# Reordering a block-sorted attention and token-mixing MLP kernel: attention of two batches one unit sooner, token units two later, an affine in single steps

## The chip, the cores and the metric

The kernel runs on one core of a Trainium2 chip. The metric is the device time of one execution in microseconds (us). A change of the order of instructions only is made; the arithmetic and the number of bytes moved are the same before and after.

## The reference

Two parts run one after the other, for 4 batches (S = 768 rows, 8 heads of 64, model width 512, hidden width 2048):

```
P = sinkhorn(sort_net, 5 rounds)                  # 8 x 8 per batch and head
k_sorted = P applied to the 8 blocks of k;  v_sorted = the same of v   # blocks of 96 rows
scores = q_b @ k_sorted_b^T / 8                   # within a block: 96 x 96
x = softmax(scores) @ v_sorted_b                  # heads side by side: 768 x 512
a1 = alpha1 * x + beta1
u  = x + lam * (w_tok @ a1)                       # mixes the 768 rows
a2 = alpha2 * u + beta2
out = u + lam * (relu(a2 @ w_ch1) @ w_ch2)
```

## The kernel before, in words

A batch b has two halves (hf = 0, 1) of three row tiles each. A half is two stages. The stage "h" is 16 units: `h_unit` is four matmuls of 128x384 (weights W1p, moving operand a2T) into one PSUM tile h_ps, which ScalarE (ACT) turns into hTa or hTb with a relu. The stage "c" is the second product. For batch 0 it is `ch_unit`, 12 pieces of four 128x512 matmuls, and for batches 1 to 3 `ch_pair`, which does two row tiles with seven products of eight 128x256 matmuls (px, py, pz, px, pz, px, py), using sums of blocks that VectorE (DVE) makes in `block_sums`. A pair gives seven steps, so the first half's stage "c" has 7 (one pair) and the second's 14 (two pairs). After each product DVE adds the PSUM tile to u into ost (`add_out`), and SP's queue sends ost out.

Everything else, for the next batch, is woven into these units and steps by hand. `put(b, hf, kind, n, f)` files a piece of work under unit or step n of a stage, and `run` issues it right behind that unit or step. All engine helpers keep program order, so the order of the `put` calls is the order of each engine's queue. With p = b - 1, the work of batch b that is filed in batch p's stages is:

- `mix_v` and `mix_k`: the block sort, as matmuls with the mixing matrix. ACT casts the results from PSUM into `mixed` and kT. `bounce_v` writes mixed to the DRAM scratch vscr and `back_v` reads it back as Vs, both on SP's queue; `loads` on POOL first copies one element of Vs (gate), so that copy waits until Vs has landed.
- `q_cross`: six DMA transposes on SP, qT from qn.
- `score` (PE: sc_ps; ACT: exp into et) and `pv` (PE: x_ps from et and Vs; DVE: reciprocal rcb, then x). Both take the two PSUM buffers of psA. After every second `pv`, two pieces go onto the list `late`: `tails` (three small copies of x) and `first_affine` (two multiplications and additions that make a). `flush` empties the list, `flush_one` issues one piece.
- `moe_tok`, the token unit: six 128x512 matmuls (w_tokT, moving operand a) into tok_ps; DVE makes u from it and ACT casts u to 16 bits. It needs all columns of a.
- `moe_cross`: three DMA transposes on SP, uT from the cast u.
- `moe_affine`: four steps that make a2T from uT, one for each 128 columns; on DVE for a batch's first half.

h_ps, tok_ps, px, py, pz and ch_ps share the four PSUM buffers of psB.

A unit, step or stage is named below by the batch whose "h" and "c" stages run: batch 1's second half, for instance, carries the token units, the mixing and the affine of batch 2.

Of the kernel before, what the change touches and what calls it, by code (L numbers as in the profile page):

```python
# [16 lines left out]
def kernel(  # L17
# [28 lines left out]
    CT = C // 128  # L46
# [28 lines left out]
    act = Engine(nc.scalar)  # L75
# [11 lines left out]
    def psa(shape, dtype, name):  # L87
        return pools["psA"].tile(shape, dtype, name=name, tag="psA")
# [390 lines left out]
    def pv(b, g, hf):  # L479
        if g == 0 and hf == 0:  # L480
            x_of[b] = moep.tile([128, 8, C], F16, name="x128", tag="x128", bufs=1)
            a1_of[b] = moep.tile([128, 8, C], F16, name="a1", tag="a1", bufs=1)
        ps = psa([128, 2, 512], FT, "x_ps")[:].rearrange("p a (k d) -> p a k d", d=128)
        et = ets[(b, g, hf)][:].rearrange("p a i t -> p (a i t)")
        for ii in range(4):
            for h2 in range(2):
                lo = (4 * h2 + ii) * BLK
                w = min(128, 8 * BLK - lo)
                pe.matmul(
                    ps[0:w, h2, ii, 0:D + 1], et[0:BLK, lo:lo + w],  # L490
                    Vs[0:BLK, (2 * g + h2) * NB + 4 * hf + ii, 0:D + 1], start=True, stop=True,
                )
        rc = att.tile([128, 2, 4], FT, name="rcb", tag="rc", bufs=3)
        dve.reciprocal(rc[0:BLK], ps[0:BLK, :, :, D])
        dve.tensor_tensor(
            x_of[b][0:BLK, 4 * hf:4 * hf + 4, g * 128:(g + 1) * 128].rearrange("p k (a d) -> p k a d", a=2),
            ps[0:BLK, :, :, 0:D].rearrange("p a k d -> p k a d"),
            rc[0:BLK].rearrange("p a k -> p k a").unsqueeze(3).to_broadcast([BLK, 4, 2, D]), ALU.mult,
        )
        if b == 1:  # L500
            flush()
        if hf == 1:
            c = slice(g * 128, (g + 1) * 128)
            late.append(lambda: tails(x_of[b], c))
            late.append(lambda: first_affine(b, slice(0, 128), slice(0, NT), c))

    late = []

    def flush():
        while late:  # L510
            late.pop(0)()

    def flush_one():
        late.pop(0)()

    def tails(x, c):
        for a in range(3):
            dve.tensor_copy(x[96:128, a:a + 4:3, c], x[32 * a:32 * a + 32, 6:8, c])
# [21 lines left out]
    def loads(b):  # L540
        pool.tensor_copy(gate[:], Vs[0:1, 0, 0:1])
        load_kv(b)
        load_q(b)
# [3 lines left out]
    def mix_v(b, n, eng):  # L547
        if n == 0:
            mixed[b] = att.tile([128, HB, D], F16, name="mixed", tag="qn" if b == B - 1 else "sums", bufs=1 if b == B - 1 else 2)
        ps = psa([128, 2, 512], FT, "mix_ps")  # L550
        raw = raw_of[(b, 1)][:].rearrange("p t d -> p (t d)")
        for m in range(2):
            pe.matmul(
                ps[:, m, :], bigM[b][:].rearrange("p a x -> p (a x)"),
                raw[:, n * 1024 + m * 512:n * 1024 + (m + 1) * 512], start=True, stop=True,
            )
        eng(
            mixed[b][:, n * 16:(n + 1) * 16, :].rearrange("p t d -> p (t d)"),
            ps[:].rearrange("p m f -> p (m f)"),
        )  # L560
# [21 lines left out]
    def bounce_v(b):  # L582
        for th in range(2):
            sp.dma_start(
                vscr[b, :, th * HB:(th + 1) * HB, :], mixed[b][th * 64:(th + 1) * 64, :, :],
            )

    def back_v(b):
        sp.dma_start(Vs[0:BLK, :, 0:D], vscr[b].rearrange("x t d -> t x d"))
# [125 lines left out]
    def moe_tok(b, kt, ps):  # L715
        u32 = u_of[b]
        tok_part(b, kt, 0, C, ps)
        if b not in u16_of:
            u16_of[b] = moep.tile([128, NT, C], F16, name="u16", tag="u16", bufs=1)
        dve.scalar_tensor_tensor(  # L720
            u32[kt], tok_of[(b, kt)][:], 1.0 / GAIN, x_of[b][:, kt, :], op0=ALU.mult, op1=ALU.add,
        )
        act.copy(u16_of[b][:, kt, :], u32[kt])

    def moe_cross(b, hf):
        uT = uT_of[(b, hf)] = att.tile([128, CT, 384], F16, name="uT", tag="uT", bufs=2)
        for m in range(3):
            sp.dma_start_transpose(
                uT[:, :, m * 128:(m + 1) * 128], u16_of[b][:, 3 * hf + m, :],
            )  # L730

    def moe_affine(b, hf):
        for ci in range(CT):
            affine(b, hf, ci, uT_of[(b, hf)][:, ci, :], act if b and hf else dve)

    uT_of = {}
# [228 lines left out]
    def put(b, hf, kind, n, *todo):  # L965
        at.setdefault((b, hf, kind, n), []).extend(todo)
# [18 lines left out]
    pairs = [("s", 0), ("s", 2), ("p", 0), ("s", 4), ("p", 2), ("s", 6), ("p", 4), ("p", 6)]  # L985
    for b in range(1, B):
        p = b - 1
        if b == 1:
            for n in range(3):
                put(0, 0, "h", 11 + n, lambda n=n: mix_v(1, n, act.copy))  # L990
                put(0, 0, "c", 3 + 3 * n, lambda n=n: mix_k(1, n, (act.copy,) * 4))
            put(0, 0, "h", 13, lambda: bounce_v(1))
            put(0, 0, "c", 1, lambda: back_v(1))
            for g in range(H4):
                put(0, 0, "c", (4, 7, 10, 10)[g], lambda g=g: q_turn_late(1, g, (dve.tensor_copy, act.copy)[g % 2]))
            put(0, 0, "c", 11, lambda: loads(2))
            seq = [("s", 0), ("s", 1), ("s", 2), ("p", 0), ("s", 3), ("p", 1), ("p", 2), ("s", 4), ("p", 3), ("s", 5),
                   ("p", 4), ("s", 6), ("p", 5), ("s", 7), ("p", 6), ("p", 7)]
            for at_, (kind, n) in enumerate(seq):
                put(0, 1, "h", at_, (lambda n=n: score(1, n // 2, n % 2, psa)) if kind == "s" else (lambda n=n: pv(1, n // 2, n % 2)))  # L1000
        else:
            for n in range(3):
                put(p - 1, 1, "c", b - 2 + n, lambda b=b, n=n: mix_v(b, n, act.copy))
                put(p - 1, 1, "c", ((4, 6, 8), (4, 7, 10))[b - 2][n], lambda b=b, n=n: mix_k(b, n, (act.copy,) * 4))
            put(p - 1, 1, "c", b, lambda b=b: bounce_v(b))
            put(p - 1, 1, "c", 7, lambda b=b: back_v(b))
            for kt in range(NT):
                put(*((0, 1, "h", 13) if b == 2 else (1, 0, "c", 1)), lambda b=b, kt=kt: q_cross(b, kt))
            if b + 1 < B:
                put(p, 0, "h", 3, lambda b=b: loads(b + 1))  # L1010
            for (kind, n), at_ in zip(
                pairs, ((0, "h", 0), (0, "h", 3), (0, "h", 5), (0, "h", 7), (0, "h", 10), (0, "c", 0), (0, "c", 4), (1, "h", 2)),
            ):
                for i in range(2):
                    f = (lambda b=b, n=n + i: score(b, n // 2, n % 2, psa)) if kind == "s" else (lambda b=b, n=n + i: pv(b, n // 2, n % 2))
                    put(p, *at_, f)
            for at_ in ((0, "h", 6), (0, "h", 7), (0, "h", 11), (0, "h", 12), (1, "h", 0), (1, "h", 1), (1, "h", 3), (1, "h", 4)):
                put(p, *at_, flush_one)
        if b == 1:
            put(p, 1, "h", 15, flush)  # L1020
        put(p, 1, "h", 3, lambda b=b: moe_start(b))
        for kt in range(3):
            put(p, 1, *(("c", 3) if b == 1 else ("h", 7 + 2 * kt)), lambda b=b, kt=kt: moe_tok(b, kt, psb))
        put(p, 1, *(("c", 3) if b == 1 else ("h", 11)), lambda b=b: moe_cross(b, 0))
        put(p, 1, "c", 8, lambda b=b: moe_affine(b, 0))
        for kt in range(3):
            put(b, 0, "h", 2 * kt, lambda b=b, kt=kt: moe_tok(b, 3 + kt, psb))
        put(b, 0, "h", 4, lambda b=b: moe_cross(b, 1))
        put(b, 0, "c", 2, lambda b=b: moe_affine(b, 1))
# [5 lines left out]
    for b in range(1, B):  # L1035
        for hf in range(2):
            for at_, lo, hi in ((8, 0, 4), (14, 4, 7), (15, 7, 8)):
                at.setdefault((b, hf, "h", at_), []).insert(0, lambda b=b, hf=hf, lo=lo, hi=hi: block_sums(b, hf, lo, hi))
        put(b, 1, "h", 11, lambda b=b: block_sums(b, 2, 0, 4))
        for at_, lo, hi in ((4, 4, 7), (6, 7, 8)):  # L1040
            put(b, 1, "c", at_, lambda b=b, lo=lo, hi=hi: block_sums(b, 2, lo, hi))

# [60 lines left out]
```

## Time and profile before

| what | value |
|---|---|
| median of 3 runs | 262.9 us (262.67 to 262.9) |
| the profiled execution | 262.66 us |
| its span, first to last instruction | 260.9 us |
| PE (matmul) busy | 248.1 us, 95% |
| DVE busy | 175.9 us, 67% |
| ACT busy | 155.0 us, 59% |
| POOL busy | 44.3 us, 17% |
| mean granted TensorE clock | 0.997 |
| moved by DMA | 31.07 MB, mean 119 GB/s |

In rows of the timeline the columns are: start in us from the span's start, length in us, engine, line, operation, result<-operands, shape, and how many instructions are merged; in brackets the engine's idle time before them and what ended it. "L65" is the line of the helper that issues every instruction, so groups are told apart by tile names. SPq is SP's DMA queue. Matmuls are pipelined: their lengths overlap, so what a matmul really costs is the distance from its start to the next one's start. In the windows, the columns are the stretch, its length, the busy time of PE, PEld, DVE, ACT and POOL, the granted clock, the DMA share and GB/s.

The stages lie so in the span: batch 0 until about 104 us; batch 1's first half 104 to 129, its second 129 to 160; batch 2's 160 to 185 and 185 to 214; batch 3 from there to the end. Batch 3 carries nothing for a later batch.

### The profile page before, as it was taken

What the parts mean: (1) busy time and instruction counts of PE and PEld (TensorE: products, weight loads), DVE (VectorE), ACT (ScalarE), POOL (GpSimd) and SP (SyncE); (2) the same over time, 40 slices, a digit from 0 to 9 for tenths busy, and PEclk for the clock granted to TensorE, in tenths of its full rate; (3) what the DMA queues carried; (4) which work ended last, traced back from release to release, by engine and by line L of the source; (5) the groups of instructions that cost most, each with busy time, mean ns of one, the idle gap of its engine ahead of it and who ended that gap; (6) DMA issues with size and microseconds to landing.
All of it is one profiled execution on the core that took longest, in us unless ns stands there. A gap on an engine that the chain in (4) does not pass through costs nothing.

```text
span 260.9 us, 5959 instructions
## 1 busy us (share of the span) xinstructions
PE 248.1 (95%) x2371; PEld 159.8 (61%) x2371; DVE 175.9 (67%) x467; ACT 155.0 (59%) x282; POOL 44.3 (17%) x67
## 2 busy tenths in 40 slices
PE   8998799999999999999989999999989989999994
PEld 2566565555555445557755797567746865685783
DVE  6696888595448846669885775298966862361873
ACT  3557667575987559796454686888345004747400
POOL 8759303600092000083000000000000000000000
PEclk9999999999999999999999999999999999999998
DMA  6999999996999976989974169610202123111022
GB/s 102 211 205 190 208 204 213 204 134 159 165 202 177 133 158 158 134 161 175 132 112 120 20 148 168 132 23 0 83 1 60 43 82 77 28 29 52 3 80 80
DMA packets 67535, 31.07 MB, mean 119 GB/s; under 512 B 56674, under 2 KB 63218, under 8 KB 67508
## 3 DMA queue, kind: packets, MB, share of 16 engines
q0 software_dynamic: 26352, 15.34, 45.6%
q1 hardware_dynamic: 41060, 15.33, 33.5%
q8 instruction: 18, 0.29, 0.5%
q14 instruction: 9, 0.07, 0.1%
q10 hardware_dynamic: 96, 0.03, 0.1%
HBM read 32.79 MB, written 8.65 MB: 159 GB/s over the span
## 4 chain that ended last, share of the span: by engine, by line
PE 71%; DVE 22%; ACT 3%; issue 2%; DVEq 0%
PE h_ps L65 20%; PE tok_ps L65 12%; DVE x L65 9%; PE ch_ps L65 8%; PE px L65 7%; PE pz L65 5%; DVE a L65 4%; PE py L65 4%; PE warm_ps L65 4%; DVE sums L65 3%; DVE ost L65 2%; PE x_ps L65 2%; PE kmix_ps L65 2%; PE mix_ps L65 2%; PE sc_ps L65 2%
## 5 line engine op out<-in xcount | busy, mean ns | idle before, releaser
L65 PE MATMUL h_ps<-a2T,W1p 128*128 128x384 bf16 x512 | 94.0, 326 | 0.0
L65 PEld LDWEIGHTS <-W1p 128*128 128x128 bf16 x512 | 48.0, 98 | 31.9 <-issue 0.4
L65 ACT ACTIVATE hTa<-h_ps 128x384 f16<-128x384 f32 x64 | 31.2, 494 | 28.0 <-PE h_ps L65 26.9
L65 ACT ACTIVATE hTb<-h_ps 128x384 f16<-128x384 f32 x64 | 31.3, 491 | 9.5 <-PE h_ps L65 9.5
L65 DVE SCALAR_TENSOR_TENSOR u<-tok_ps,x 128x512 f32<-128x512 f32 x21 | 14.5, 691 | 27.7 <-PE tok_ps L65 27.7
L65 PE MATMUL tok_ps<-a,w_tokT 128*128 128x512 f16 x126 | 30.3, 379 | 1.8 <-DVE a L65 1.8
L65 ACT CAST kT<-kmix_ps 64x512 f16<-64x512 f32 x36 | 25.7, 715 | 4.9 <-PE kmix_ps L65 4.2
L65 ACT CAST u<-u 128x512 f16<-128x512 f32 x21 | 13.0, 619 | 24.5 <-DVE u L65 24.5
L65 ACT ACTIVATE et<-sc_ps 96x768 f16<-96x768 f32 (+1 forms) x32 | 24.8, 810 | 3.4 <-PE sc_ps L65 3.4
L65 PEld LDWEIGHTS <-sums 128*128 128x128 f16 x216 | 21.1, 98 | 5.2 <-issue 2.1
L65 PEld LDWEIGHTS <-hTb 128*128 128x128 f16 x200 | 18.6, 98 | 6.3
L65 PEld LDWEIGHTS <-hTa 128*128 128x128 f16 x192 | 18.4, 98 | 6.3
L65 PEld LDWEIGHTS <-w_tokT 128*128 128x128 f16 x126 | 12.2, 98 | 15.3 <-DVE a L65 2.5
L65 DVE TENSOR_TENSOR x<-x_ps,rcb 96x512 f16<-96x512 f32 x24 | 16.5, 686 | 0.8
L65 POOL DMA_DIRECT2D qn<-in_q_dram x18 | 16.0, 905 | 3.8 <-DMA raw<-in_v_dram 3.3
L65 DVE TENSOR_TENSOR sums<-hTa,hTb 128x512 f16<-128x512 f16 (+2 forms) x27 | 8.9, 329 | 10.0 <-ACT hTb L65 10.0
L65 PEld LDWEIGHTS <-et 96*128 96x128 f16 (+4 forms) x288 | 11.9, 100 | 5.6 <-DVE x L65 2.6
L65 PE MATMUL x_ps<-Vs,et 96*128 96x65 f16 (+4 forms) x288 | 13.0, 195 | 2.2 <-DVE x L65 1.4
L65 DVE SCALAR_TENSOR_TENSOR ost<-px,u 128x256 f32<-128x256 f32 x27 | 11.3, 418 | 3.1 <-PE px L65 3.1
L65 PE MATMUL warm_ps<-wz 128*128 128x512 f16 x36 | 11.9, 466 | 1.2 <-DVE wz L65 1.2
L65 PE MATMUL ch_ps<-W2p,hTa 128*128 128x512 f16 x48 | 12.0, 379 | 0.0
L65 PE MATMUL ch_ps<-W2p,hTb 128*128 128x512 f16 x48 | 12.0, 379 | 0.0
(139 smaller groups left out, 349.7 us busy)
## 6 DMA issues: line engine op xcount, KB each, us to landing
out_dram<-ost SPq DMA_DIRECT2D x23, 192.0 KB, 2.5
raw<-in_v_dram POOLq DMA_DIRECT2D x6, 384.0 KB, 7.0
raw<-in_k_dram POOLq DMA_DIRECT2D x6, 384.0 KB, 9.8
qn<-in_q_dram POOLq DMA_DIRECT2D x18, 128.0 KB, 10.1
vscr<-mixed SPq DMA_DIRECT2D x6, 384.0 KB
Vs<-vscr SPq DMA_DIRECT2D x3, 768.0 KB
W1p<-in_moe_w_ch_dram POOLq DMA_DIRECT2D x4, 512.0 KB, 11.3
W2p<-in_moe_w_ch_dram POOLq DMA_DIRECT2D x4, 512.0 KB, 17.2
```

Source lines behind the costliest of these rows:

```text
L65: ins = getattr(self.eng, name)(*args, **kwargs)
```

## The change

Order only; no instruction is added or taken away.

- `pv` of batch 1 issues one late piece behind each of its x steps, where it issued all that were waiting.
- The V mixing of batch 2 goes to steps 1, 2, 3 of batch 0's second half (it was 0, 1, 2), and its bounce to step 3 (it was 2). For batch 3 these places stay what they were.
- For batches 2 and 3, four of the score and pv groups, and four of the single late pieces, go one unit sooner in the stage "h" of the batch before, first half.
- The first three token units of batches 2 and 3 go from units 7, 9, 11 to 9, 11, 13, their transposes from unit 11 to 13.
- The four steps of the first affine of batches 2 and 3 go to steps 8, 9, 10, 11, one each (they were all at step 8). For batch 1 all four stay at step 8.
- One group of block sums goes from unit 11 to 12.

```
-        if b == 1:
-            flush()
+        if b == 1 and late:
+            flush_one()
...
-    def moe_affine(b, hf):
-        for ci in range(CT):
+    def moe_affine(b, hf, cis=range(CT)):
+        for ci in cis:
             affine(b, hf, ci, uT_of[(b, hf)][:, ci, :], act if b and hf else dve)
...
-                put(p - 1, 1, "c", b - 2 + n, lambda b=b, n=n: mix_v(b, n, act.copy))
+                put(p - 1, 1, "c", 1 + n, lambda b=b, n=n: mix_v(b, n, act.copy))
...
-            put(p - 1, 1, "c", b, lambda b=b: bounce_v(b))
+            put(p - 1, 1, "c", 3, lambda b=b: bounce_v(b))
...
-                pairs, ((0, "h", 0), (0, "h", 3), (0, "h", 5), (0, "h", 7), (0, "h", 10), (0, "c", 0), (0, "c", 4), (1, "h", 2)),
+                pairs, ((0, "h", 0), (0, "h", 2), (0, "h", 4), (0, "h", 6), (0, "h", 9), (0, "c", 0), (0, "c", 4), (1, "h", 2)),
...
-            for at_ in ((0, "h", 6), (0, "h", 7), (0, "h", 11), (0, "h", 12), (1, "h", 0), (1, "h", 1), (1, "h", 3), (1, "h", 4)):
+            for at_ in ((0, "h", 5), (0, "h", 6), (0, "h", 10), (0, "h", 11), (1, "h", 0), (1, "h", 1), (1, "h", 3), (1, "h", 4)):
...
-            put(p, 1, *(("c", 3) if b == 1 else ("h", 7 + 2 * kt)), lambda b=b, kt=kt: moe_tok(b, kt, psb))
-        put(p, 1, *(("c", 3) if b == 1 else ("h", 11)), lambda b=b: moe_cross(b, 0))
-        put(p, 1, "c", 8, lambda b=b: moe_affine(b, 0))
+            put(p, 1, *(("c", 3) if b == 1 else ("h", 9 + 2 * kt)), lambda b=b, kt=kt: moe_tok(b, kt, psb))
+        put(p, 1, *(("c", 3) if b == 1 else ("h", 13)), lambda b=b: moe_cross(b, 0))
+        for ci in range(CT):
+            put(p, 1, "c", 8 if b == 1 else 8 + ci, lambda b=b, ci=ci: moe_affine(b, 0, (ci,)))
...
-        put(b, 1, "h", 11, lambda b=b: block_sums(b, 2, 0, 4))
+        put(b, 1, "h", 12, lambda b=b: block_sums(b, 2, 0, 4))
```

## The prediction

> **What bounds the kernel now.** I read the page first. TensorE (PE) is busy 95% of the span, VectorE (DVE) 67%, ScalarE (ACT) 59%, and the chain that ended last is 71% PE and 22% DVE: PE bounds it, except where PE stands behind a DVE result. All this change does is reorder, so the question is which holes of PE it closes. I then asked for PE's waits in the stages that the diff touches, and for the timeline and the windows around each hole.
>
> ```profile
> PE 248.1 (95%) x2371; PEld 159.8 (61%) x2371; DVE 175.9 (67%) x467; ACT 155.0 (59%) x282; POOL 44.3 (17%) x67
> PE 71%; DVE 22%; ACT 3%; issue 2%; DVEq 0%
> ```
>
> The first hole, batch 1's second half (the same at 187.26 to 191.55 in batch 2's):
>
> ```profile
> 131.86 3.42 PE L65 MATMUL h_ps<-a2T,W1p 128*128 128x384 bf16 x20
> 134.95 0.56 DVE L65 TENSOR_TENSOR a<-x,alphaB 128x768 f16<-128x768 f16 x1
> 135.54 0.56 DVE L65 TENSOR_TENSOR a<-a,betaB 128x768 f16<-128x768 f16 x1
> 136.15 1.04 PE L65 MATMUL tok_ps<-a,w_tokT 128*128 128x512 f16 x4 [0.88 <-DVE a L65]
> ...
> 131.86:136.15 4.29, 3.42 (x25) 1.86 (x21) 4.00 (x11) 2.69 (x6) 0.00 (x0) 1.00 0.70 87
> 187.26:191.55 4.29, 3.42 (x26) 1.86 (x21) 4.00 (x11) 2.70 (x6) 0.00 (x0) 1.00 0.13 42
> ```
>
> The reader sees PE finish units 3 to 7, then stand until the last piece of a, the token units' input, is written at 136.10. In the two windows (columns: stretch, length, busy PE, PEld, DVE, ACT, POOL) PE works 3.42 of 4.29 us, DVE 4.00: DVE sets the end of this stretch.
>
> The second hole, batch 2's last output pair:
>
> ```profile
> 208.51 1.04 PE L65 MATMUL pz<-TWa,sums 128*128 128x256 f16 x8
> 209.38 1.04 PE L65 MATMUL px<-TWa,sums 128*128 128x256 f16 x8
> 209.38 0.42 DVE L65 SCALAR_TENSOR_TENSOR ost<-py,ost 128x256 f32<-128x256 f32 x1
> 209.73 1.24 DVE L65 TENSOR_SCALAR a2T<-uT,ab2col 128x384 bf16<-128x384 f16 x4
> 210.88 0.42 DVE L65 SCALAR_TENSOR_TENSOR ost<-pz,u 128x256 f32<-128x256 f32 x1
> 211.35 0.38 PE L65 MATMUL pz<-W2p,sums 128*128 128x256 f16 x2 [0.93 <-DVE ost L65]
> ```
>
> PE may not add to pz before DVE has read it, and that read is queued behind the four affine steps.
>
> The stage where the diff could cost something, batch 2's start (K's casts, then the SP queue's own view, then the first use of Vs):
>
> ```profile
> 97.11 8.73 ACT L65 CAST kT<-kmix_ps 64x512 f16<-64x512 f32 x12
> 93.75 1.18 SPq L65 DMA_DIRECT2D vscr<-mixed  x2
> 95.02 3.05 SPq L65 DMA_DIRECT2D out_dram<-ost  x2
> 98.16 3.82 SPq L65 DMA_TRANSPOSE uT<-u  x3
> 103.17 0.37 SPq L65 DMA_DIRECT2D Vs<-vscr  x1
> 111.73 0.18 POOL L65 COPY gate<-Vs 1x1 f16<-1x1 f16 x1 [30.51 <-DMA Vs<-vscr]
> ```
>
> **Token units two later (batches 2, 3).** No instruction is added. A unit is four 128x384 matmuls; 16 of them take 2.60 us in the chain, so 0.1625 us each and 0.65 a unit. Unit 7 ends by start-to-start at 131.86 + 20 x 0.1625 = 135.11; the token unit starts at 136.15, so 1.04 us are lost. Now units 8 and 9 (1.30 us) come first: PE reaches the token unit at 136.41, when a is 0.3 us old. The whole 1.04 goes, twice: **2.08 us**. (Here the row and the Trainium skill differ: by "Perfetto Trace Analysis", Per-engine timelines, Tensor Engine Instruction, the end of a matmul is estimated and not observed, so an idle time that starts at such an end is too short. By the idle column this term would be 0.88 + 0.87 = 1.75 us, by starts 2.08.) What is late next: the last token unit's DVE step (0.69 us) and its ACT cast (0.62) come closer to the pair, but DVE is busy 5.47 of 9.40 us in 136.0 to 145.4. Its three transposes on SP (139.03 to 145.41) end up to about 1 us later against the pair; their reader is at 155.84 in batch 1 and 209.73 in batch 2, some 6 to 10 us behind. Cost zero, and 1 us per us if that margin were gone.
>
> **Affine in four single steps.** The same four instructions. Four take 1.24 us and one 0.374 us, so they start (1.24 - 0.374) / 3 = 0.29 apart. With one step ahead of it the read of pz starts at 209.73 + 0.29 = 210.02, ends at 210.44, and PE resumes 0.05 later (as 210.88 + 0.42 to 211.35), at 210.49 instead of 211.35. px ends by starts at 209.38 + 0.87 = 210.25, so 0.24 of the hole stays: **0.86 us** gained in batch 2's last pair. (The skill's "VectorE: DVE Perf Modes", The DRAIN you can't avoid, says that the next DVE step does not start until the pipe is empty; starts 0.29 apart with 0.374 long do not agree. By it the read would come at 210.10 and the gain be 0.78.) Steps 2 to 4 fall behind later reads; the last lies behind the second read of pz, done near 212.3, before the next batch's unit 0 at 213.97 - 0.86 = 213.1. In batch 1's last pair a K mix (157.04 to 157.49) fills PE while the four steps run: gain 0.
>
> **Attention one unit sooner (batches 2, 3).** The scores, the products with Vs and their flushes keep their DVE order. In these stages DVE is the one that is full: 10.67 of 11.27 us from 113.73 on, 10.68 of 11.29 from 169.46, each stretch opened by the first product with Vs after 0.2 us of idle. The product now stands ahead of a unit, so at most that 0.22 is won at the opening. At the end PE waits for DVE's ost, 0.51 us in batch 1's pair, 0.35 by starts in batch 2's. Against it: the scores now meet PSUM buffers that ACT's exp or DVE's x frees a little later (110.25 and 115.5 as the rows stand), so PE loses up to 0.4 where it has slack. I take **0.2 + 0.1**. Bounds: one unit lost in each batch (-0.65 each) to the whole waits (+0.51, +0.35).
>
> **Batch 1 in single pieces, batch 2's V mix a step later.** DVE's copies and a steps no longer stand in one block ahead of the next x. PE's two waits for an x buffer (0.51 us at 81.20, 0.51 at 85.39, starts 0.67 and 0.4 late) go, so PE comes into the output stage some 1 us sooner. But the token units there wait for the last a: DVE does the same steps, only without its 0.53 and 0.52 idle, and ends near 90.7 instead of 91.43. Then the third V cast (1.01 us) moves on ACT from before the three u casts to behind them, ahead of the 12 K casts: they start 0.9 sooner and 1.0 later, end near 105.8 as now (105.84), and the first score needs all 12. **0**; bounds -0.4 (the waits stay, K is late, partly absorbed by the wait for exp) and +0.7. On SP the V bounce leaves behind the u transposes now: those wait for casts near 96.1 and end about 97.3, so vscr leaves about 97.3 instead of 93.75. In batch 2's stage Vs left 5.75 us after vscr (151.28 to 157.03), which gives 103.1 here against 103.17 now: Vs lands as before and is first read near 112.7. Cost zero; each us that it lands after 112.7 costs one.
>
> **Sum.** 2.08 + 0.86 + 0.3 + 0 = 3.24 us. The profiled execution took 262.66 us (span 260.9, 1.8 around it): 259.4. The runs' median, 262.9, lies 0.24 above it: 259.7. I say **259.5**.
>
> **Rivals.**
> - *Batch 2's start eats part.* The kT casts or the exps on ACT set the first scores, and PE loses 0.4 to 0.65 in one or both attention stages: gain 2.08 + 0.86 - 1.3 = 1.6, **261.0**. For it: kT is full on ACT for 8.73 us. Against: PE has 0.5 us of slack at the end of that stage.
> - *The holes only move.* PE reaches the pair 1 us sooner and waits there for DVE's sums and the last token step: 0.3 + 0.86 left, **261.5**. Against: DVE is 42% idle between token unit and pair, and its sums wait for ACT's h, which come sooner too.
> - *Vs comes late: slower.* Place: the first product with Vs of batch 2 (113.27 now). If SP drains as slowly as before, uT ends at 101.99 and vscr leaves at 102.0. From vscr's issue to the gate it was 14.2 us in batch 1's bounce (57.71, gate 71.88), 18.0 here (93.75 to 111.73): Vs would land at 116.2 to 120.0, and PE and DVE stand until then. Middle 118.1: 4.8 us late against 113.27, less the 2.94 of the two holes and 0.1: 262.66 + 4.8 - 3.04 = **264.4**. It decides from a landing at 116.3. Against: SP's late transposes came after vscr and a 3.05 us out; both are now behind them.
> - *No change of order where it counts* is excluded for PE: the built program has units 8 and 9 ahead of the token unit.
>
> **How the numbers follow.** Forecast 0.62 (own range 258.6 to 260.3: the bounds of the start and of the attention stages); part eaten 0.15 (261.0); holes move 0.11 (261.5); Vs late 0.10 (264.4; of it 0.02 for landings that only cancel the gain); 0.02 for a cancelling sum of small losses. Two tenths may lie outside: 258.6 to 261.5, which leaves out the Vs case and the edges. A difference of 0.2% (0.5 us) is what a measurement here can tell from none. The first three cases are all faster by more: 0.88; same 0.04; slower 0.08.
>
> **What would show it.** Right: no PE wait for DVE a of 0.9 us ahead of the token units in the second halves; PE's wait for pz in the last pair of batch 2 down to 0.2 to 0.3; PE's time from the first token unit to the pair unchanged. The V bounce's gate near 111 to 112, and kT's last cast near 105.8. Wrong: a gate after 113, a new wait of px, py or pz for DVE ost in the last pairs, a wait of sc_ps for ACT of over half a us, or a2T waiting for uT.

## The result, and the profile after

| | before | after |
|---|---|---|
| median of 4 runs each | 262.9 us (262.67 to 263.05) | 259.32 us (258.79 to 259.7) |
| ratio, 95% interval | | 0.9863 [0.9844, 0.9882] |
| the profiled execution (its span) | 262.66 us (260.9) | 258.79 us (257.0) |

The changed kernel is faster by 1.4%, 3.6 us. The forecast was 259.5 us, with a range of 258.6 to 261.5.

The page of after: the busy time of the engines, and the chain that ended last by engine and by tile.

```profile
PE 246.4 (96%) x2371; PEld 159.7 (62%) x2371; DVE 176.3 (69%) x467; ACT 155.3 (60%) x282; POOL 44.2 (17%) x67
PE 75%; DVE 10%; DMA 7%; ACT 4%; issue 2%; SPq 1%; DVEq 0%; POOLq 0%
PE h_ps L65 27%; PE tok_ps L65 10%; PE px L65 8%; PE pz L65 6%; PE py L65 6%; DVE x L65 5%; PE ch_ps L65 4%; PE x_ps L65 3%; DMA Vs<-vscr 3%; PE warm_ps L65 2%; DMA vscr<-mixed 2%; PE sc_ps L65 2%; DMA q<-in_q_dram 2%; DVE a L65 2%; PE v_ps L65 1%
```

DVE's share of the chain falls from 22% to 10%, and 7% of DMA come in: 5 of them are the bounce of V (vscr, then Vs), which was nowhere in the chain before.

The first hole, in the timeline of batch 1's second half, and the windows around it and around its twin in batch 2's:

```profile
130.97 4.72 PE L65 MATMUL h_ps<-a2T,W1p 128*128 128x384 bf16 x28
134.66 0.56 DVE L65 TENSOR_TENSOR a<-a,betaB 128x768 f16<-128x768 f16 x1
135.52 1.46 PE L65 MATMUL tok_ps<-a,w_tokT 128*128 128x512 f16 x6
...
130.97:135.52 4.55, 4.55 (x34) 2.74 (x30) 4.32 (x12) 3.08 (x7) 0.00 (x0) 1.00 1.41 142
185.33:189.88 4.55, 4.55 (x33) 2.73 (x30) 4.32 (x12) 3.09 (x7) 0.00 (x0) 1.00 0.14 40
```

PE is now busy in all of the 4.55 us (it was 3.42 of 4.29); a is ready at 135.22, 0.3 us before the token unit at 135.52, which no longer waits.

The second hole, batch 2's last output pair:

```profile
206.40 1.04 PE L65 MATMUL px<-TWa,sums 128*128 128x256 f16 x8
206.73 0.37 DVE L65 TENSOR_SCALAR a2T<-uT,ab2col 128x384 bf16<-128x384 f16 x1
207.02 0.42 DVE L65 SCALAR_TENSOR_TENSOR ost<-pz,u 128x256 f32<-128x256 f32 x1
207.35 0.37 DVE L65 TENSOR_SCALAR a2T<-uT,ab2col 128x384 bf16<-128x384 f16 x1
207.49 1.03 PE L65 MATMUL pz<-W2p,sums 128*128 128x256 f16 x8
```

Only one affine step stands ahead of the read of pz. PE's products px and pz start 1.09 us apart; undisturbed it is 0.87, so 0.22 of the hole is left.

Batch 2's start, which by its places runs in batch 0's last output stage and batch 1's first half (ACT's casts of K, the SP queue, the first score, the first use of Vs):

```profile
90.34 4.04 PE L65 MATMUL tok_ps<-a,w_tokT 128*128 128x512 f16 x18 [0.53 <-DVE a L65]
93.67 1.00 SPq L65 DMA_DIRECT2D out_dram<-ost  x2
94.76 3.81 SPq L65 DMA_TRANSPOSE uT<-u  x3
96.58 8.76 ACT L65 CAST kT<-kmix_ps 64x512 f16<-64x512 f32 x12
98.66 1.18 SPq L65 DMA_DIRECT2D vscr<-mixed  x2
...
104.50 0.32 SPq L65 DMA_DIRECT2D Vs<-vscr  x1
105.06 0.85 PE L65 MATMUL sc_ps<-qT,kT 64*128 64x96 f16 x16
...
112.37 0.69 PE L65 MATMUL x_ps<-Vs,et 96*128 96x65 f16 x16 [0.16 <-DMA Vs<-vscr]
112.45 0.18 POOL L65 COPY gate<-Vs 1x1 f16<-1x1 f16 x1 [30.93 <-DMA Vs<-vscr]
```

The rows of before that go with these, the last of them the wait at the end of the stage:

```profile
91.71 4.05 PE L65 MATMUL tok_ps<-a,w_tokT 128*128 128x512 f16 x18
106.19 0.51 PE L65 MATMUL sc_ps<-qT,kT 64*128 64x96 f16 x16
113.27 0.68 PE L65 MATMUL x_ps<-Vs,et 96*128 96x65 f16 x16
125.39 1.03 PE L65 MATMUL px<-TWa,sums 128*128 128x256 f16 x8 [0.51 <-DVE ost L65]
```

The token units come at 90.34 instead of 91.71. The last cast of kT ends at 105.34, inside the first score, whose row grew from 0.51 to 0.85 us; in before it ended at 105.84, 0.35 us ahead of the score. PE has begun to wait for Vs.

For the split of the gain, the span is cut at rows of PE that both kernels have: unit 0 of batch 0's second half (U0), unit 0 of batch 1's first half (U1), the second px of its pair (P1, the product that waited 0.51 us for ost), and unit 0 of batches 1's second (U2), 2's first (U3), 2's second (U4) and 3's first half (U5). Distances by starts, us, from the profiled run of each kernel, those of the experiments included:

| kernel | to U0 | U0-U1 | U1-P1 | P1-U2 | U2-U3 | U3-U4 | U4-U5 | U5-end |
|---|---|---|---|---|---|---|---|---|
| before | 70.00 | 33.84 | 21.55 | 4.01 | 30.71 | 24.69 | 29.17 | 46.91 |
| after | 69.67 | 33.23 | 21.60 | 4.01 | 29.66 | 24.70 | 27.24 | 46.90 |
| after, again | 70.13 | 33.05 | 22.04 | 4.00 | 29.66 | 24.70 | 27.24 | 46.88 |
| e1 tokens only | 69.81 | 34.20 | 21.61 | 4.00 | 29.66 | 24.71 | 28.11 | 46.94 |
| e2 affine only | 69.57 | 33.72 | 21.99 | 4.01 | 30.72 | 24.69 | 28.31 | 46.93 |
| e3 attention only | 69.54 | 34.31 | 22.33 | 4.00 | 30.72 | 24.70 | 29.17 | 46.89 |
| e4 batch 1 only | 71.94 | 33.04 | 21.77 | 4.00 | 30.73 | 24.69 | 29.18 | 46.90 |
| e5 without attention | 69.33 | 33.03 | 21.72 | 4.01 | 30.23 | 24.70 | 27.24 | 46.91 |
| e6 mix early | 69.55 | 33.26 | 22.16 | 4.00 | 29.67 | 24.69 | 27.24 | 46.89 |
| e7 affine at 9 | 70.40 | 33.18 | 21.75 | 4.01 | 29.66 | 24.69 | 27.03 | 46.93 |
| e8 bounce late | 69.42 | 33.05 | 22.92 | 4.01 | 29.66 | 24.70 | 27.24 | 46.90 |
| e9 tokens at 8 | 69.39 | 33.20 | 22.50 | 4.00 | 30.07 | 24.70 | 28.04 | 46.89 |
| e10 gate late | 69.44 | 34.81 | 21.86 | 4.01 | 29.68 | 24.70 | 27.24 | 46.95 |
| e11 best | 70.27 | 33.04 | 21.51 | 4.01 | 29.66 | 24.70 | 27.03 | 46.91 |

The code before U0 is the same in all of them and its time varies by 1.1 us even without e4's 71.94, so the 0.33 us there are not the change's. From U2 on the stages repeat to 0.02 us where the kernels are the same (the last one to 0.08), but for U2-U3 of e5; there a row decides alone. Between U0 and P1, with its DMA traffic, kernels that are the same there scatter by more: U0-P1 is 54.83 in after and 55.70 in e9, and U0-U1 is 33.26 in e6 and 34.81 in e10.

### The profile page after: what moved, and what is told of

It reads as the page before. It is cut to its first block, busy times and chain, and to the rows that moved or that the text cites. A ratio compares the mean times of both kernels' runs of the same rounds, so it can differ in the third digit from the quotient of the medians.

```text
span 257.0 us, 5959 instructions
## 1 busy us (share of the span) xinstructions
PE 246.4 (96%) x2371; PEld 159.7 (62%) x2371; DVE 176.3 (69%) x467; ACT 155.3 (60%) x282; POOL 44.2 (17%) x67
## 4 chain that ended last, share of the span: by engine, by line
PE 75%; DVE 10%; DMA 7%; ACT 4%; issue 2%; SPq 1%; DVEq 0%; POOLq 0%
PE h_ps L65 27%; PE tok_ps L65 10%; PE px L65 8%; PE pz L65 6%; PE py L65 6%; DVE x L65 5%; PE ch_ps L65 4%; PE x_ps L65 3%; DMA Vs<-vscr 3%; PE warm_ps L65 2%; DMA vscr<-mixed 2%; PE sc_ps L65 2%; DMA q<-in_q_dram 2%; DVE a L65 2%; PE v_ps L65 1%
## 5 line engine op out<-in xcount | busy, mean ns | idle before, releaser
L65 PE MATMUL warm_ps<-wz 128*128 128x512 f16 x36 | 11.0, 439 | 1.2 <-DVE wz L65 1.2
L65 ACT CAST mixed<-mix_ps 128x1024 f16<-128x1024 f32 x9 | 9.1, 1012 | 4.7 <-PE mix_ps L65 4.5
```

The lines of the kernel that those rows point to most:

```text
L65: ins = getattr(self.eng, name)(*args, **kwargs)
```

## The experiments

Times are medians in us, each beside the kernel before of its own call; its median was 263.51 in the first call (e1 to e4), 262.52 in the second (after again, e5, e6, e7) and 263.43 in the third (e8 to e11), so calls are compared by ratio. The ratio is the one on record; it is not the quotient of the two medians (for e2 that would be 0.9937, for e4 0.9959).

**e1: the token units alone** (on the kernel before)

```
-("h", 7 + 2 * kt)   moe_cross ("h", 11)   block_sums(b, 2, 0, 4) at "h", 11
+("h", 9 + 2 * kt)   moe_cross ("h", 13)   block_sums(b, 2, 0, 4) at "h", 12
```

> The kernel before with only the token units of batches 2 and 3 at units 9, 11, 13 (their transposes at 13, the block sums at 12). Theory A (the two holes before the token units close by themselves): 2 x 1.04 = 2.1 us less, 260.8. Rival B (the holes close only because the attention work ahead of them also comes sooner): under 1.3 us less. Rival C (the holes move to the output pair): under 0.5 us less.

Measured: 261.32, ratio 0.9913 [0.9885, 0.9941]. U2-U3 falls by 1.05 us and U4-U5 by 1.06: the two holes, and nothing is given back before the next batch.

**e2: the affine alone** (on the kernel before)

```
-put(p, 1, "c", 8, lambda b=b: moe_affine(b, 0))
+for ci in range(CT): put(p, 1, "c", 8 if b == 1 else 8 + ci, ... moe_affine(b, 0, (ci,)))
```

> The kernel before with only the affine of batches 2 and 3 in four single steps. Theory A: PE's hole before the second pz product of batch 2's last pair shrinks from 1.10 to 0.24 by starts, 0.86 us less, 262.0; nothing in batch 1's last pair, where a K mix fills PE. Rival: the later steps push the reads of px back and the wait moves there: 0 to 0.3 less.

Measured: 261.84, ratio 0.9925 [0.9905, 0.9945]. U4-U5 falls by 0.86 us, U2-U3 by nothing. The ratio says 2.0 us, the medians 1.7; the trace shows 0.86 in the only stage that the edit touches, and the trace is taken.

**e3: the attention alone** (on the kernel before)

```
-score, pv at "h", 0 3 5 7 10     flush_one at "h", 6 7 11 12
+score, pv at "h", 0 2 4 6 9      flush_one at "h", 5 6 10 11
```

> The kernel before with only scores, products with Vs and their flushes of batches 2 and 3 one unit sooner. The forecast: 0.2 + 0.1 = 0.3 us less, 262.6. Rival (the sooner scores stand before PSUM buffers that are not free, and PE loses up to 0.65 in each batch): 0.3 to 1.3 us more, up to 264.2. Rival (VectorE's stretch opens 0.2 sooner and PE's closing waits of 0.5 and 0.35 go entirely): 0.85 less, 262.05.

Measured: 263.27, ratio 0.9988 [0.9974, 1.0003]: no difference that can be told, and the interval holds the forecast's 0.3 us as well as nothing. The stages say more: U3-U4 is 24.70 against 24.69. In batch 2's start PE's waits from 104 to 136 us are more, not fewer, than before, where there was only the one for ost of 0.5:

```profile
PE sc_ps L65 <- ACT et L65: 0.5, 2, 0.4
PE sc_ps L65 <- DVE x L65: 0.4, 1, 0.4
PE px L65 <- DVE ost L65: 0.3, 1, 0.3
PE h_ps L65 <- DVE a2T L65: 0.2, 1, 0.2
```

The scores, one unit sooner, find their PSUM buffers still held by exp and by x. In this profile two of DVE's copies of x also took 0.60 and 0.62 us beside POOL's q issues, where one took 0.55 in before (see e10), so the 22.33 of U1-P1 is not the move's alone.

**e4: batch 1's single pieces, with the later V mix and bounce** (on the kernel before)

```
-if b == 1: flush()                     mix_v at b - 2 + n     bounce_v at b
+if b == 1 and late: flush_one()        mix_v at 1 + n         bounce_v at 3
```

> The kernel before with only batch 1's late pieces issued one by one and batch 2's V mixing and bounce one step later. The forecast: 0 (bounds 0.4 more to 0.7 less). From the trace of the changed kernel: PE is 0.9 us sooner at the output stage, and 0.6 of it is still there at batch 2's first pair, so 0.3 to 0.6 less, 262.3 to 262.6. Rival (Vs lands about 0.7 later and PE pays it): 0.3 more.

Measured: 262.42, ratio 0.9936 [0.9912, 0.9959]. U0-U1 is 33.04 against 33.84, 33.72, 34.20 and 34.31 in the four kernels that keep the block flush. So this part, which I had put at nothing, is worth a good half microsecond; by the medians the run is 1.1 us faster. Which share is the single pieces' and which the later mix's, e4 alone does not show (see e6).

The four ratios add up to 2.4% where the whole change is worth 1.4%. They share one set of runs of before, whose median of 263.51 is 0.2% above the first 262.9 and goes into the sum four times; that can make most of the excess, but it isn't shown that it does. The split therefore rests on the stages, not on these ratios.

**After, again** (the changed kernel, for the second call)

> The changed kernel again, as the mark for the runs beside it: 0.986 of the kernel before, about 3.5 us less.

Measured: 258.65, ratio 0.9861 [0.9836, 0.9887], as at first.

**e5: after without the attention move**

```
-score, pv at "h", 0 2 4 6 9      flush_one at "h", 5 6 10 11
+score, pv at "h", 0 3 5 7 10     flush_one at "h", 6 7 11 12
```

> The changed kernel with the attention work of batches 2 and 3 back at its old units. Theory A (VectorE sets these stages, one unit changes little): within 0.3 us of the changed kernel. Forecast's term: 0.3 more. Rival (the sooner attention is what makes the token input ready): over 1 us more.

Measured: 258.95, ratio 0.9862 [0.9838, 0.9885], like after's 0.9861. Nothing is lost without it. In the profiled run it lost 0.57 us between U2 and U3 that after did not lose, nor e1 and e11, which also have the old units: ACT's a2T waited 3.15 us for uT there (1.94 in after), and PE for a2T.

**e6: the V mix and its bounce of batch 2 early again, the rest as after**

```
-mix_v at 1 + n         bounce_v at 3
+mix_v at b - 2 + n     bounce_v at b
```

> The changed kernel with batch 2's V mixing at steps 0, 1, 2 and its bounce at 2 again; vscr then leaves SP's queue ahead of the three transposes, near 94, and Vs near 103. If the 0.16 us that PE waited for Vs and the one V cast behind the u casts cost what they seem to: 0.2 to 0.6 us less than the changed kernel. Rival (the early mixing stands in PE's way before x buffers are free, and the token units' input sets the end anyway): 0 to 0.4 more.

Measured: 259.77, ratio 0.9896 [0.9871, 0.9921], 1.1 us above after in the same call; the intervals overlap a little. The profile shows 0.3 to 0.6 of it between U0 and P1 (55.42, after's two have 54.83 and 55.09), which is inside the scatter there. What its rows say: vscr leaves at 92.77, with an out of 3.06 us behind it, and the transposes of u start at 97.20 instead of 94.76. So PE, which now comes sooner, waits 0.5 us for a2T ahead of U1. After U1 the gate falls at 110.67, and POOL's issues come beside DVE's copies (e10). What the later place buys is on SP: the transposes go ahead of the bounce. The mix itself costs nothing where it was: the token units start 20.50 us after U0 here, with all three mixes ahead of them, and 20.67 in after, with two. The early mix with the late bounce was not run.

**e7: after with the four affine steps one step later**

```
-put(p, 1, "c", 8 if b == 1 else 8 + ci, ...)
+put(p, 1, "c", 8 if b == 1 else 9 + ci, ...)
```

> The changed kernel with the affine steps of batches 2 and 3 at steps 9 to 12 instead of 8 to 11, so that the first read of pz stands ahead of all of them. If the 0.22 us that stay of the hole are the one affine step ahead of that read: 0.2 us less than the changed kernel, and pz starts right behind px. Rival (the last affine step is now late for the next batch's unit 0): 0 to 0.5 more.

Measured: 259.0, ratio 0.9855 [0.9829, 0.9882]. The last pair of batch 2, timeline:

```profile
207.23 1.04 PE L65 MATMUL px<-TWa,sums 128*128 128x256 f16 x8
207.57 0.41 DVE L65 SCALAR_TENSOR_TENSOR ost<-pz,u 128x256 f32<-128x256 f32 x1
207.90 0.37 DVE L65 TENSOR_SCALAR a2T<-uT,ab2col 128x384 bf16<-128x384 f16 x1
208.10 1.04 PE L65 MATMUL pz<-W2p,sums 128*128 128x256 f16 x8
```

With no step ahead of the read of pz, px and pz start 0.87 us apart and the rest of the hole is gone: U4-U5 is 27.03, 0.21 less. So the cause of the second hole is the place of the read in DVE's queue, step by step: four ahead cost 1.1 us, one costs 0.2, none costs none.

**e8: after with the bounce of batch 2 later still**

```
-put(p - 1, 1, "c", 3, lambda b=b: bounce_v(b))
+put(p - 1, 1, "c", 7 if b == 2 else 3, lambda b=b: bounce_v(b))
```

> The changed kernel with batch 2's V bounce at step 7, so that on SP it stands behind the out transfers of the second piece. vscr leaves near 101.2 instead of 98.7, Vs 5.8 later near 107, and lands near 114.9 instead of 112.4. The rival's price (one us for each us that Vs lands after 112.7): 2.2 to 2.5 us more than the changed kernel, 261.0 to 261.9. Other view (the stages behind have slack that takes it up): under 1 us more.

Measured: 259.65, ratio 0.9858 [0.9829, 0.9887]. The timeline:

```profile
100.36 1.10 SPq L65 DMA_DIRECT2D vscr<-mixed  x2
105.60 0.34 SPq L65 DMA_DIRECT2D Vs<-vscr  x1
113.28 0.69 PE L65 MATMUL x_ps<-Vs,et 96*128 96x65 f16 x16 [1.50 <-DMA Vs<-vscr]
113.35 0.18 POOL L65 COPY gate<-Vs 1x1 f16<-1x1 f16 x1 [32.20 <-DMA Vs<-vscr]
```

The out that stood ahead took only 0.79 us this time, so the gate fell only 0.9 us later than after's and the test is weaker than planned. From U1 to the gate it is 10.88 against 9.55, 1.33 later, and U1-P1 is 22.92 against 21.60, 1.32 longer; from the first product with Vs to P1 it is 12.1 in both. So between these two profiles a late Vs costs one for one, as the rival's price said. The other runs scatter around this: after's second run and e9 gave 9.75 and 10.14 with 22.04 and 22.50. The times don't show the price: e8's ratio is after's (0.9858, 0.9861), where 1.3 us would be 0.005, and by them the other view (under 1 us) holds. In the profiled run U0-U1 and the start were on the short side; what the other runs did there isn't known.

**e9: after with the token units one unit sooner**

```
-("h", 9 + 2 * kt)   moe_cross ("h", 13)
+("h", 8 + 2 * kt)   moe_cross ("h", 12)
```

> The changed kernel with the token units of batches 2 and 3 at units 8, 10, 12, one unit later than before instead of two (transposes at 12). One unit covers 0.65 of the 1.04 us: PE should wait about 0.4 us for a in each of the two second halves, 0.7 to 0.8 us more than the changed kernel in all. Rival (the holes were closed by what stands ahead, not by the two units): no difference.

Measured: 260.59, ratio 0.9895 [0.9871, 0.9919]. In batch 1's second half (timeline), then PE's waits from 191 to 215 us:

```profile
135.24 0.56 DVE L65 TENSOR_TENSOR a<-a,betaB 128x768 f16<-128x768 f16 x1
135.85 1.47 PE L65 MATMUL tok_ps<-a,w_tokT 128*128 128x512 f16 x6 [0.23 <-DVE a L65]
```

```profile
PE px L65 <- DVE ost L65: 0.2, 1, 0.2
PE tok_ps L65 <- DVE a L65: 0.2, 1, 0.2
```

One unit (0.65) of the 1.04 is covered and the rest, 0.41 in U2-U3, stays, as the arithmetic of units says. U4-U5 loses 0.80: again 0.4 for a, and another 0.4 that comes later, at the wait of px for ost: 0.2 in the idle column, 0.40 by starts (px at 202.08, 1.27 behind pz, undisturbed 0.87).

**e10: e6 with POOL's loads for batch 3 held back until the first half's step 0**

```
-put(p, 0, "h", 3, lambda b=b: loads(b + 1))
+put(p, 0, "c", 0, lambda b=b: loads(b + 1))     # and its gate waits for batch 2's a, not for Vs
```

> The changed kernel with the early V mixing, and with POOL's loads for batch 3 held until batch 2's second group of a is written, so that POOL issues no DMA beside the copies of x in batch 1's first half. Theory (VectorE's copies of x are stretched from 0.22 to about 0.6 us when POOL issues a DMA, and this stage is bound by VectorE): the first three copies take 0.7 us together instead of 1.3, and from the first product with Vs to the second px product it is 12.1 instead of 12.7 us. Rival (the stretch has another cause): the copies stay at 1.3 us. The later loads may collide with later copies, so the time of the whole may stay.

Measured: 260.15, ratio 0.9872 [0.9838, 0.9907]. The three copies of x behind the first product with Vs, and POOL's row, in e6 and then here:

```profile
113.40 4.42 POOL L65 DMA_DIRECT2D qn<-in_q_dram  x5
114.82 1.30 DVE L65 COPY x<-x 32x256 f16<-32x256 f16 x3
```

```profile
116.26 0.69 DVE L65 COPY x<-x 32x256 f16<-32x256 f16 x3
123.43 0.18 POOL L65 COPY gate<-a 1x1 f16<-1x1 f16 x1 [41.48 <-DVE a L65]
```

With POOL silent the copies are back at 0.69. From the product to P1 it is 12.45 us against 12.74 in e6 (and 12.13 in after; 12.1 was expected): half of what the copies lost comes back. The run as a whole did not gain: with the early bounce, SP's transposes of u started at 98.64 here and PE waited 2.0 us for a2T ahead of U1, which has nothing to do with the gate.

**e11: the version that the runs point to** (after with the edits of e5 and e7)

> The changed kernel with the affine steps at 9 to 12 and with the attention work of batches 2 and 3 at its old units. By the traces of the two alone: 0.2 us less for the affine, 0.0 to 0.2 less for the attention: 0.2 to 0.4 us less than the changed kernel.

Measured: 259.12, ratio 0.9837 [0.9808, 0.9866]. Its stages are the shortest of all kernels or level with them (U1-P1 21.51, U4-U5 27.03), 0.2 us of which is the affine's; by time it can't be told from after (0.9861).

## Why the prediction was right, point by point

- **Token units, 2.08 us: right.** 1.05 in U2-U3 and 1.05 of the 1.93 in U4-U5; e1 shows them alone and e9 that unit 8 would not have been enough. From the first token unit to U3 it was 23.96 us and is 22.65; with the two units moved ahead of it (1.30) that is the same, so nothing fell late behind them. The rival "holes only move" is refuted. The wait column (0.88 and 0.87) was too short for both; the sum by starts was the better one.
- **Affine, 0.86 us: right.** 0.86 alone in e2, 0.88 in after. 0.24 of the hole was to stay, 0.22 did. The rule of the Trainium skill ("VectorE: DVE Perf Modes", The DRAIN you can't avoid), by which the gain would have been 0.78, does not fit as the prediction took it: in after the read of pz starts 0.29 us after a step that is 0.37 long. The section itself goes on that a next step which is not held starts earlier, which the prediction left out; the row agrees with that.
- **Attention, 0.3 us: wrong, it is worth nothing in batch 3's start, and in batch 2's it costs some 0.3 us.** The win at the end came as forecast: the wait of px for ost is gone in both batches. The step that failed is the balance at the opening: I counted 0.2 as won there and allowed a loss only "where it has slack". Batch 3's start (batch 2's first half, U3-U4) in before and in after:

```profile
169.00 0.68 PE L65 MATMUL x_ps<-Vs,et 96*128 96x65 f16 x16
177.28 1.04 PE L65 MATMUL px<-W2p,hTa 128*128 128x256 f16 x8
180.80 1.03 PE L65 MATMUL px<-TWa,sums 128*128 128x256 f16 x8 [0.18 <-DVE ost L65]
```

```profile
166.41 0.68 PE L65 MATMUL x_ps<-Vs,et 96*128 96x65 f16 x16
169.03 0.34 PE L65 MATMUL sc_ps<-qT,kT 64*128 64x96 f16 x8 [0.36 <-DVE x L65]
175.68 1.04 PE L65 MATMUL px<-W2p,hTa 128*128 128x256 f16 x8
178.86 1.04 PE L65 MATMUL px<-TWa,sums 128*128 128x256 f16 x8
```

The first product with Vs does come 0.65 sooner after U3 (8.24 against 8.89), but the next score then waits for x (0.4), so the pair starts 0.34 later after U3 (17.51 against 17.17), and what the pair won back is just that. One wait took the place of another, since DVE's work in the stage is what it was: from its first step on that product to its first step for the pair 10.85 us, before 10.87. In batch 2's start the first product came no sooner after U1 (9.47 against 9.43): kT held the first score, exp the second, Vs the product. After's waits from 104 to 136 us, where before had only the 0.5 for ost:

```profile
PE sc_ps L65 <- ACT et L65: 0.3, 1, 0.3
PE x_ps L65 <- DMA Vs<-vscr: 0.2, 1, 0.2
```

Since Vs sets that product, the move puts one more unit behind it: from the product to P1 it is 12.1 us with the move (after, e7, e8) and 11.85 without (e4, e5, e11). After's second run and e9 have 12.4, and in each a copy of x was stretched, to 0.51 and 0.58 us. With batch 1's edits in and the mix as in after, U0-P1 is 54.81, 54.75 and 54.55 without the move (e4, e5, e11) and 54.83, 55.09, 54.93 and 55.70 with it (after twice, e7, e9).
- **Batch 1's pieces and the later mix, 0: mis-sized, upwards.** Without the attention move U0-P1 is 54.70 on average against 55.64 in the kernels with the block flush and no attention move (before, e1, e2: 55.39, 55.81, 55.71): some 0.9 us (0.6 to 1.3 between single profiles), above my bound of 0.7. What I said of the pieces held: a is ready at 90.29, forecast near 90.7, and PE comes into the token units 1.04 us sooner, counted from U0. (Of the forecast's two waits for an x buffer, the 0.51 at 85.39 is the weight load's row; PE itself started 0.3 late there, not 0.4.) That is the pieces' doing: in e6, with the third V mix still ahead of them, it comes 1.22 sooner, and in after the place of that mix (0.43) is a wait for a (0.53). What failed is the end of the step: that the first score needs all 12 casts of kT and takes all of it back. kT hardly moved, as forecast (35.67 us after U0, it was 35.84). But before, the score had started 0.35 behind the last cast's end, so that much was free, and in after it started at 105.06, 0.3 ahead of that end, and only its later matmuls waited: 0.3 lost of 0.6.
- **Vs, no cost: mis-sized; it lands as forecast, but no room is left.** vscr left at 98.66, not 97.3: I had let the transposes of u start with their casts, but an out of 1.00 us stood ahead of them and the three took 3.81 one behind the other. From vscr to Vs it was 5.84 us (5.75 taken). The gate came at 112.45, forecast 111 to 112. I had PE at the first product with Vs at 112.7; it was there at 112.2, since U1 comes 0.94 us sooner, and waited 0.16 us. In all the kernels with the later bounce the first product starts at the landing, 0.08 us ahead of the gate, and PE stands idle ahead of it: 0.2 to 0.7 us, and 1.5 in e8 (for three of them the profile names ACT's hTa, but the start follows the landing). In e4, e5 and e9 the landing was 0.4 to 0.6 us later after U1 than in after. So this rival is there, at some tenths of a microsecond; e8 shows its price.

The parts against the forecast, in the profiled pair: 2.10 (2.08), 0.88 (0.86), batch 2's start 0.56 and batch 3's 0.0 (0.3 + 0 for both), sum 3.54 (3.24); the 0.33 that the profiled pair shows beyond that lies ahead of all changed code. That the sum came out so close is in part luck: an attention term too high stood beside a batch 1 term too low.

## What to carry to other kernels

A hole of a busy engine was closed in full here where work that was ready was put ahead of the waiting instruction and the late result had room behind it; the size of such a hole is the distance of starts less the undisturbed distance, not the idle column. Moving a producer sooner in a stage where another engine is full closed none here: ask which buffer the moved work now needs and who still holds it. Where one queue carries several transfers, put first the one whose reader is next (here the transposes ahead of the bounce), and read how much room the other one has left before moving it again.

## What the runs showed of the hardware that was not expected

DVE's copies of 32x256 16-bit values take 0.22 us, except beside POOL's DMA issues. The group of them in after (shortest/median/longest in ns):

```profile
L65 DVE COPY x<-x x36: 219/220/627, 77.8 to 188.2; 32x256 f16<-32x256 f16 x36
```

In e6, the three copies behind the first product with Vs took 1.30 us while POOL issued the q loads, and 0.69 in e10 where POOL was silent. Not every copy beside an issue is stretched, and the 14 profiles show which are. Of their 504 copies, 41 took over 0.23 us, the longest 0.745 (e5). Each of these began 0.24 to 0.74 us after the start of one of POOL's DMA issues (0.88 to 0.95 us long for q, 0.55 for raw) and ended 0.02 to 0.05 us after that issue's end. Copies that began in the first 0.21 us of an issue took 0.22. The Trainium skill ("SBUF — State Buffer", Who interferes with whom) says that copies can use a port pair that DVE shares with GpSimd, and that whoever comes second is blocked for the whole of the other's instruction. The rows fit that for the later part of an issue: such a copy stands until the issue is over. Why the first 0.2 us of an issue block nothing, they don't show.
